# Seven half products in three more places, and the first loads written into the order

## The chip, the cores and the metric

The kernel runs on one core of one Trainium2 chip. The metric is the device time of one execution in microseconds (us), median of the runs. A core has TensorE (PE, the matmuls and the loads of their weights), VectorE (DVE), ScalarE (ACT) and GpSimd (POOL, which here only issues DMAs), each working through its own instructions in program order, and SyncE (SP), which issues the other DMAs. Data goes from DRAM to SBUF and back by DMA; matmuls write to PSUM, which has eight banks of 128 partitions by 2 KB.

## The reference

Two stages. First attention over a short window with a few global positions (4 batches, 8 heads, 768 positions, head size 64):

```python
scores = scale * np.matmul(q, k.transpose(0, 1, 3, 2))
keep = is_global | is_local          # column < 8, or 0 <= row - column < 96
bias = -slopes[:, None, None] * dist[None, :, :]
a = softmax(np.where(keep, scores + bias, -1e9))
attn = np.matmul(a, v)               # written [batch * position, head * 64]: 3072 x 512
```

Then two matrix products with a squared ReLU between them:

```python
h = x @ w_in                         # 3072 x 512 times 512 x 2048
g = np.maximum(h, 0.0) ** 2
out = g @ w_out                      # 3072 x 2048 times 2048 x 512
```

## The kernel before

**Tiles and blocks.** The 3072 positions are 24 tiles of 128 (index j) and 12 blocks of two tiles (blk). A tile needs of attention only itself, the tile in front of it and the global positions. All matmuls are in bf16.

**One tile of attention.** `tr.n.j` and `T.n.j` transpose q (n = 0) and k (n = 1) by PE and copy them out of PSUM (tiles 0 to 5); from tile 6 on one `T.j` does both as a DMA transpose issued by SP. `bias`, `sc.j.g` (scores, in two groups of heads), `exp.j.odd.g` (ACT), `mul.j.odd.g` (DVE, times a table of biases), `pv.j.hf` (PE, times v) and `norm.j.hf` (DVE) follow. `gk`, `gv` and `kl` copy the global positions. The normed tile is transposed for the second stage by `trx.j` and `xT.j` (tiles 0 to 7, PE and a copy) or by `xT.j` alone (from tile 8, a DMA transpose by SP).

**Stage 1 of a block.** `s1.blk.s` for s = 0 to 7 gives 256 of the 2048 hidden columns for both tiles: eight matmuls of 256 columns (one per token of the block) into one bank. `relu.blk.s` (ACT) and `sq.blk.s` (ACT or DVE) follow; in the list, @A and @V name the engine.

**Stage 2 of a block.** Plain (`s2.blk.s.sub`): for each step s and tile of the block two matmuls of 512 columns. In blocks 2 to 10 it is done as seven half products instead, function `seven`: the product is seen as a 2 x 2 product of blocks (two tiles, two halves of each pair of hidden columns, two halves of the 512 output columns). Four sums of the squared activations (`sum.blk.i`, DVE) and four sums of weights (`wsum.i.g`, DVE, made once) let seven products `p1` to `p7` of 8 matmuls of 256 columns stand for eight. They gather in two banks, x and y, of a ring of two (`ps_acc`); `part.blk.p` copies between products, and `o.blk.p` write the output tile, which `st.blk.sub` stores (SP). Block 11 is plain, with its last tile cut at column 384.

**PSUM.** Two banks are the ring `ps_acc`; six are the ring `ps_g` (named g, the score ring) which scores, transposes and stage 1 share in turn.

**Loads.** POOL issues them through `swdge` (line 258), in one queue. q, k and v come as float32 and land as bf16. Thirty-four first loads (tiles 1 to 5, v of tile 0, and all weights: `i` is `win`, `o` is `wout`) are issued by one loop ahead of everything else, from a string in the kernel:

```python
for w in "q1 k1 k3 v0 q2 k2 v1 q3 v2 i0 i1 v3 i2 i3 q4 o0 k5 k4 i4 o1 v4 i5 q5 i6 o2 i7 o3 o4 o5 v5 o6 o7".split():
    pieces[w[0]](int(w[1:]))
```

Behind them come `load.6` to `load.23` (q, k and v of one tile each); `gate.8` to `gate.10` are tiny writes by DVE that hold back the load of the same number.

**What sets the order.** The list ORDER holds one word per piece of work. `Plan.run` emits the pieces in the order of the list, and so it fixes, for every engine and queue, in which order it does its own. The costs and keys given to `plan.op` change nothing of that. Waits between engines follow from the data.

Of the kernel before, what the change touches and what calls it, by code (L numbers as in the profile page):

```python
# [11 lines left out]
FP32 = mybir.dt.float32  # L12
# [42 lines left out]
tr.0.0 T.0.0@A tr.1.0 tr.0.1 T.0.1@A bias.0.0 tr.1.1 T.1.0@V T.1.1@A sc.0.0 bias.1.0 exp.0.0.0 sc.1.0 exp.0.1.0  # L55
bias.1.1 exp.1.0.0 exp.1.1.0 pv.0.0 pv.0.1 norm.0.0 norm.0.1 sc.1.1 tr.0.2 tr.1.2 gk.1 tr.1.3 exp.1.0.1 exp.1.1.1
T.1.2@V bias.2.0 T.0.2@V pv.1.0 T.1.3@A sc.2.0 trx.0 exp.2.0.0 pv.1.1 bias.2.1 xT.0@V exp.2.1.0 tr.0.3 T.0.3@A sc.2.1
gk.2 sc.3.0 exp.2.0.1 sc.3.1 exp.2.1.1 exp.3.0.0 exp.3.1.0 exp.3.1.1 norm.1.0 norm.1.1 trx.1 gv.1 pv.2.0 mul.3.0.0
xT.1@V pv.2.1 s1.0.0 s1.0.0#2 exp.3.0.1 norm.2.0 norm.2.1 mul.3.1.0 gv.2 s1.0.1 mul.3.1.1 relu.0.0 pv.3.0 mul.3.0.1
relu.0.1 pv.3.1 sq.0.0@A s1.0.2 trx.2 norm.3.0 norm.3.1 s1.0.2#2 xT.2@V trx.3 xT.3@A sq.0.1@V gk.3 relu.0.2 s1.0.3  # L60
ones.6 load.6 sq.0.2@V relu.0.3 s1.1.0 sq.0.3@A relu.1.0 E0.1 E0.0 sq.1.0@V s1.1.1 relu.1.1 sq.1.1@V tr.0.4 tr.1.5
s1.1.2 s1.1.3 tr.1.4 T.0.4@A relu.1.2 s2.0.0.0 T.1.5@A s2.0.0.1 sq.1.2@A relu.1.3 sq.1.3@A T.1.4@V sc.4.1 sc.4.0
exp.4.1.1 s1.0.4 s1.1.4 exp.4.0.1 relu.1.4 relu.0.4 s1.0.5 gv.3 mul.4.1.1 exp.4.0.0 sq.0.4@V mul.4.0.0 T.6 s1.1.5
s2.0.1.0 exp.4.1.0 mul.4.1.0 mul.4.0.1 tr.0.5 sq.1.4@A pv.4.0 T.0.5@V s2.0.1.1 pv.4.1 relu.0.5 gk.4 norm.4.0 s2.0.2.0
norm.4.1 load.7 relu.1.5 sc.5.0 exp.5.1.0 sc.5.1 mul.5.1.0 s1.1.7 s2.0.2.1 gv.4 s1.0.6 exp.5.0.0 exp.5.0.1 sq.0.5@A
s1.0.7 sq.1.5@A s1.1.6 s2.0.3.1 s2.0.4.1 s2.0.3.0 relu.1.7 sq.1.7@V wsum.0.0 wsum.1.0 mul.5.0.0 relu.0.7 sq.0.7@A
exp.5.1.1 trx.4 mul.5.0.1 mul.5.1.1 relu.0.6 sq.0.6@A relu.1.6 s2.0.4.0 pv.5.0 xT.4@A s2.0.5.1 wsum.2.0 norm.5.0
s2.0.5.0 pv.5.1 s2.0.6.0 norm.5.1 s2.0.7.0 o.0.0@A s2.0.6.1 s2.0.7.1 trx.5 s2.1.0.1 s2.1.1.1 s2.1.2.1 s2.1.3.1 xT.5@V
sq.1.6@A s1.2.0 st.0.0 s2.1.4.1 gate.8 wsum.0.1 relu.2.0 T.7 wsum.3.0 wsum.2.1 sq.2.0@V load.8 s1.2.2 relu.2.2 s1.2.4
sq.2.2@A s2.1.5.1 s2.1.6.1 o.0.1@V s2.1.7.1 relu.2.4 s1.2.5 relu.2.5 o.1.1@V sc.6.0 exp.6.0.0 st.1.1 exp.6.1.0 s1.2.1  # L70
s2.1.0.0 s1.2.3 sq.2.5@V sq.2.4@A sc.7.0 relu.2.1 st.0.1 mul.6.0.0 sc.7.1 mul.6.1.0 gate.9 exp.7.0.0 s2.1.1.0 s2.1.2.0
s2.1.3.0 T.8 exp.7.1.1 s1.2.7 gk.7 mul.7.0.0 wsum.1.1 wsum.3.1 relu.2.3 mul.7.1.1 exp.7.1.0 mul.7.1.0 load.9 exp.7.0.1
mul.7.0.1 sq.2.1@A pv.6.0 sq.2.3@A relu.2.7 pv.6.1 sq.2.7@A s1.2.6 relu.2.6 s2.1.4.0 s2.1.5.0 load.11 pv.7.1 pv.7.0
norm.6.0 norm.6.1 s2.1.6.0 trx.6 s2.1.7.0 s2.2.p1.0 o.1.0@A norm.7.0 norm.7.1 trx.7 sq.2.6@V xT.6@A xT.7@A T.9 sc.8.1
sc.8.0 sum.2.0 sum.2.1 s2.2.p2.0 exp.8.1.1 exp.8.0.0 s2.2.p1.1 exp.8.0.1 gate.10 s1.3.2 load.10 mul.8.1.1 s1.3.0
sum.2.2 exp.8.1.0 s1.3.4 relu.3.0 part.2.p1@V s2.2.p6.0 mul.8.0.0 mul.8.1.0 s2.2.p2.1 gv.7 pv.8.0 mul.8.0.1 relu.3.2
sq.3.0@V pv.8.1 s2.2.p6.1 norm.8.0 s1.3.1 norm.8.1 gk.8 part.2.p6@A relu.3.4 sq.3.2@A o.2.p2 relu.3.1 xT.8 s2.2.p7.0
s2.2.p5.0 s2.2.p5.1 gv.8 sum.2.3 sc.9.1 sc.9.0 s2.2.p7.1 exp.9.0.1 sq.3.4@V s1.3.5 sq.3.1@V mul.9.0.1 load.12
exp.9.1.1 gk.9 s1.3.3 exp.9.1.0 mul.9.1.1 exp.9.0.0 part.2.p7@V T.10 s2.2.p4.0 T.11 load.13 mul.9.1.0 relu.3.5
relu.3.3 sq.3.3@A pv.9.1 mul.9.0.0 pv.9.0 sq.3.5@V norm.9.0 norm.9.1 s1.3.6 s1.3.7 relu.3.6 o.2.p5 sq.3.6@V s2.2.p4.1  # L80
s2.2.p3.0 relu.3.7 s2.2.p3.1 o.2.p4@V gv.9 sq.3.7@A s2.3.p1.0 s2.3.p1.1 xT.9 o.2.p3 sum.3.0 s2.3.p2.0 st.1.0 sum.3.1
s2.3.p2.1 sc.10.0 sc.10.1 exp.10.0.1 exp.10.0.0 part.3.p1@V o.3.p2 s2.3.p6.0 s2.3.p6.1 s2.3.p5.0 mul.10.0.1 mul.10.0.0
T.12 gk.10 exp.10.1.1 s2.3.p5.1 mul.10.1.1 exp.10.1.0 s1.4.0 relu.4.0 mul.10.1.0 s1.4.6 sum.3.2 pv.10.0 pv.10.1
norm.10.0 sc.11.0 relu.4.6 exp.11.1.0 norm.10.1 xT.10 sq.4.0@V s1.4.7 s1.4.5 load.14 mul.11.1.0 part.3.p6@V sc.12.0
exp.11.0.0 load.15 relu.4.7 sq.4.6@A sum.3.3 mul.11.0.0 sc.11.1 s2.3.p7.0 relu.4.5 exp.11.1.1 exp.11.0.1 sq.4.7@V
mul.11.1.1 s2.3.p7.1 exp.12.0.0 gv.10 exp.12.1.0 part.3.p7@V s1.4.3 T.13 mul.11.0.1 s1.4.2 pv.11.0 mul.12.1.0 pv.11.1
s1.4.1 mul.12.0.0 norm.11.0 relu.4.3 norm.11.1 sq.4.5@A pv.12.0 s1.4.4 xT.11 sq.4.3@A norm.12.0 s2.3.p4.0 relu.4.2
sq.4.2@A s2.3.p4.1 pv.12.1 relu.4.1 st.2.1 relu.4.4 o.3.p5 sq.4.1@V o.3.p4@A s2.3.p3.0 sq.4.4@A st.2.0 s2.3.p3.1
load.16 s2.4.p1.0 norm.12.1 o.3.p3 sum.4.0 s2.4.p1.1 sum.4.1 part.4.p1@V s2.4.p2.0 s2.4.p2.1 sc.13.0 exp.13.1.0
sc.13.1 exp.13.0.0 mul.13.1.0 s2.4.p6.0 s2.4.p6.1 mul.13.0.0 part.4.p6@A exp.13.1.1 exp.13.0.1 sum.4.2 xT.12 s1.5.2  # L90
s1.5.0 s2.4.p7.0 pv.13.0 s2.4.p7.1 T.14 relu.5.0 mul.13.1.1 st.3.0 part.4.p7@A mul.13.0.1 o.4.p2 relu.5.2 s1.5.5
sq.5.0@V s2.4.p5.0 s1.5.3 relu.5.3 sq.5.3@A sq.5.2@V pv.13.1 s1.5.1 s1.5.7 s2.4.p4.0 s2.4.p5.1 st.3.1 norm.13.0 s1.5.4
norm.13.1 relu.5.5 xT.13 sum.4.3 sq.5.5@A T.15 gk.13 s1.5.6 o.4.p5 relu.5.7 gv.13 s2.4.p4.1 relu.5.1 sq.5.7@A sq.5.1@V
relu.5.4 relu.5.6 sq.5.4@A s2.4.p3.0 s2.4.p3.1 load.17 o.4.p4@V s2.5.p1.0 sc.14.1 kl.14 sq.5.6@A load.18 sc.14.0
exp.14.1.0 o.4.p3 s2.5.p1.1 s2.5.p2.0 s2.5.p2.1 sum.5.0 sum.5.1 part.5.p1@A exp.14.0.0 s2.5.p6.0 sum.5.3 mul.14.0.0
exp.14.0.1 mul.14.1.0 s2.5.p6.1 s1.6.0 exp.14.1.1 o.5.p2 T.16 part.5.p6@A pv.14.0 s2.5.p5.0 sum.5.2 relu.6.0 s1.6.6
mul.14.0.1 s2.5.p7.0 relu.6.6 norm.14.0 mul.14.1.1 pv.14.1 norm.14.1 xT.14 sc.15.0 sc.15.1 s1.6.7 s2.5.p5.1 s2.5.p7.1
s1.6.4 sq.6.0@A load.19 exp.15.1.0 kl.15 mul.15.1.0 gv.14 exp.15.0.1 mul.15.0.1 exp.15.0.0 mul.15.0.0 exp.15.1.1
mul.15.1.1 sq.6.6@A part.5.p7@V o.5.p5 relu.6.7 pv.15.0 pv.15.1 norm.15.0 relu.6.4 sq.6.7@A s2.5.p4.0 sc.16.1 sc.16.0
norm.15.1 xT.15 gv.15 exp.16.0.1 gk.16 s2.5.p4.1 s1.6.1 s1.6.3 s1.6.2 s2.5.p3.0 exp.16.1.1 exp.16.1.0 st.4.0 T.17  # L100
relu.6.1 mul.16.0.1 mul.16.1.1 mul.16.1.0 sq.6.4@V exp.16.0.0 mul.16.0.0 pv.16.0 s1.6.5 pv.16.1 s2.5.p3.1 sq.6.1@V
relu.6.3 T.18 s1.7.1 relu.6.2 sq.6.3@A relu.6.5 norm.16.0 o.5.p4@A sq.6.2@V s1.7.0 s2.6.p1.0 sq.6.5@A o.5.p3 st.5.0
s2.6.p1.1 sum.6.0 norm.16.1 xT.16 sum.6.1 load.20 relu.7.0 part.6.p1@A s2.6.p2.0 s2.6.p2.1 relu.7.1 s2.6.p6.0 st.4.1
s2.6.p6.1 sc.17.0 sq.7.0@V sc.17.1 sum.6.2 part.6.p6@A T.19 sc.18.0 o.6.p2 s2.6.p7.0 s2.6.p7.1 exp.17.1.1 exp.17.0.0
s2.6.p5.0 s2.6.p5.1 s1.7.3 exp.17.0.1 sq.7.1@V mul.17.1.1 gv.16 exp.17.1.0 part.6.p7@V sum.6.3 relu.7.3 mul.17.0.0
st.5.1 mul.17.1.0 exp.18.0.0 o.6.p5 s1.7.5 pv.17.0 s2.6.p4.0 mul.17.0.1 s2.6.p4.1 pv.17.1 exp.18.1.0 mul.18.0.0
norm.17.0 mul.18.1.0 s2.6.p3.0 o.6.p4@A s2.6.p3.1 s1.7.4 norm.17.1 xT.17 sq.7.3@V relu.7.5 pv.18.1 sq.7.5@V s1.7.2
pv.18.0 s1.7.6 relu.7.2 norm.18.0 s1.7.7 sq.7.2@V load.22 s2.7.p1.0 relu.7.4 load.21 o.6.p3 sq.7.4@A s2.7.p2.0
norm.18.1 relu.7.7 relu.7.6 sq.7.7@V sq.7.6@A xT.18 sum.7.0 sc.19.1 kl.19 sc.19.0 s1.8.0 exp.19.1.0 mul.19.1.0 T.20
exp.19.1.1 exp.19.0.1 s2.7.p1.1 s1.8.1 s2.7.p2.1 s1.8.2 part.7.p1@A mul.19.0.1 sum.7.1 s2.7.p6.0 s2.7.p6.1 s1.8.4  # L110
st.6.1 sum.7.2 st.6.0 T.21 o.7.p2 exp.19.0.0 mul.19.1.1 mul.19.0.0 pv.19.1 pv.19.0 s2.7.p5.0 relu.8.0 sq.8.0@V
relu.8.1 part.7.p6@V s2.7.p7.0 s1.8.5 s1.8.6 s2.7.p7.1 relu.8.2 sq.8.2@A sq.8.1@V load.23 relu.8.4 norm.19.0 s2.7.p5.1
# [27 lines left out]
def kernel(  # L140
# [13 lines left out]
    P = 128  # L154
# [73 lines left out]
    STEP = {(4, 0): -7, (12, 0): 37, (5, 0): -2, (10, 0): 29, (13, 0): 30, (23, 1): 81}  # L228
    JGATE = 11
    NHB = 3  # L230
    SEVEN = set(range(2, 11))
    SQA = {3, 6}
    NSUM = 2
    NAT = 8
# [5 lines left out]
    LEAD = 12  # L240


    land = {}
    issue = [1.35, 4.6]

    def landed(name, at):
# [914 lines left out]
```

## Time and profile before

| | us |
|---|---|
| median of 3 runs | 207.66 (206.72 to 208.12) |
| the profiled execution | 206.5 |
| its span, first to last instruction | 204.7 |
| PE busy | 197.9 (97%) |
| DVE busy | 146.5 (72%) |
| ACT busy | 142.8 (70%) |
| first matmul of stage 1 (s1.0.0) | 16.55 |
| first matmul of s2.0.6.0, which needs wout 6 | 40.79 |
| last matmul ends | 201.3 |

Times in the profile count from the first instruction of the span. The page names groups by line, engine and operation, with out<-in in the program's names; "x8" is eight instructions. The chain of waits goes back from the last instruction to what released each step. A busy PE there includes the running out of the pipeline after the last matmul, so the start-to-start distances in the chain are the better price of a matmul. Granted clock is the TensorE clock that the throttle let through; it is 1.00 in every stretch.

### The profile page before, as it was taken

How to read it: one execution, taken by the hardware profiler on the slowest of the kernel's cores; microseconds unless marked ns; L12 is line 12 of the kernel's file. 1: busy time of each engine (PE TensorE's matmuls, PEld its weight loads, DVE VectorE, ACT ScalarE, POOL GpSimd, SP SyncE). 2: the span in 40 equal slices, each digit the busy share in tenths (PEclk: the TensorE clock that was granted, in tenths of full speed). 3: DMA queues.
4: the chain of work that ended last, by engine and by line, in shares of the span. 5: the costliest groups of instructions: out<-in, count | busy, mean ns of one | idle time of the engine just before them, and what ended most of it. 6: DMA issues, size and time to landing. Idle time of an engine off the chain costs nothing.

```text
span 204.7 us, 5515 instructions
## 1 busy us (share of the span) xinstructions
PE 197.9 (97%) x2200; PEld 162.6 (79%) x2200; DVE 146.5 (72%) x394; ACT 142.8 (70%) x277; POOL 75.3 (37%) x93
## 2 busy tenths in 40 slices
PE   7988999999999999999999999999999999999993
PEld 3667976657679888888988898989888888989851
DVE  8269736855788997987577978869698778747331
ACT  6986988835986847976787976576859587744330
POOL 8999866540639049150316305180500000000000
PEclk9999999999999999999999999999999999999999
DMA  8999999999999999969997999999985212120032
GB/s 127 151 172 183 182 188 205 181 154 178 213 122 111 166 138 151 153 127 144 191 140 72 108 228 142 164 117 239 145 124 80 52 74 83 29 102 0 5 115 90
DMA packets 113676, 27.36 MB, mean 134 GB/s; under 512 B 105330, under 2 KB 110706, under 8 KB 113650
## 3 DMA queue, kind: packets, MB, share of 16 engines
q0 software_dynamic: 80256, 13.37, 93.5%
q1 hardware_dynamic: 33394, 13.64, 35.3%
q8 instruction: 17, 0.28, 0.5%
q14 instruction: 9, 0.07, 0.1%
HBM read 27.26 MB, written 6.29 MB: 164 GB/s over the span
## 4 chain that ended last, share of the span: by engine, by line
PE 86%; POOL 5%; DVE 3%; DMA 2%; ACT 2%; issue 0%; POOLq 0%; ACTq 0%
PE hT L813 39%; PE acc L951 27%; PE acc L1068 10%; PE sc L538 5%; PE po L691 5%; POOL qk L258 3%; DMA win<-in_moe_w_in_dram 2%; POOL v L258 1%; ACT hr L836 1%; DVE at L629 1%; POOL win L258 1%; PE trx L759 1%; DVE v L739 1%; DVE x L722 0%; ACT esc L604 0%
## 5 line engine op out<-in xcount | busy, mean ns | idle before, releaser
L813 PE MATMUL hT<-xT,win 128*128 128x256 bf16 x768 | 94.4, 273 | 0.1
L813 PEld LDWEIGHTS <-win 128*128 128x128 bf16 x768 | 73.5, 98 | 10.4 <-issue 0.2
L836 ACT ACTIVATE hr<-hT 128x512 f32<-128x512 f32 x96 | 56.3, 602 | 31.1 <-PE hT L813 27.1
L604 ACT ACTIVATE esc<-sc 128x512 bf16<-128x512 f32 x78 | 42.0, 607 | 10.4 <-PE sc L538 10.1
L258 POOL DMA_DIRECT2D qk<-in_q_dram x23 | 20.9, 908 | 65.9 <-DMA qkT<-qk 49.9
L854 DVE TENSOR_TENSOR hs<-hr 128x512 bf16<-128x512 f32 x46 | 31.1, 685 | 9.7 <-ACT hr L836 9.6
L629 DVE TENSOR_TENSOR at<-esc,E 128x512 bf16<-128x512 bf16 x78 | 31.3, 419 | 7.1 <-ACT esc L604 6.1
L852 ACT ACTIVATE hs<-hr 128x512 bf16<-128x512 f32 x50 | 31.1, 635 | 0.7
L951 PEld LDWEIGHTS <-hsum 128*128 128x128 bf16 x288 | 27.0, 98 | 3.5
L951 PE MATMUL acc<-wsum,hsum 128*128 128x256 bf16 x216 | 28.9, 273 | 0.0
L1068 PE MATMUL acc<-wout,hs 128*128 128x512 bf16 (+2 forms) x112 | 24.0, 349 | 0.0
L951 PEld LDWEIGHTS <-hs 128*128 128x128 bf16 x216 | 20.6, 98 | 3.0
L258 POOL DMA_DIRECT2D v<-in_v_dram x24 | 21.9, 913 | 1.0 <-DMA win<-in_moe_w_in_dram 0.6
L722 DVE TENSOR_TENSOR x<-po,rs 128x256 bf16<-128x256 f32 x48 | 20.4, 425 | 1.9 <-DVE rs L721 0.2
L258 POOL DMA_DIRECT2D qk<-in_k_dram x23 | 20.6, 901 | 0.7 <-DMA win<-in_moe_w_in_dram 0.4
L951 PE MATMUL acc<-wout,hs 128*128 128x256 bf16 x144 | 18.9, 273 | 0.0
L691 PE MATMUL po<-v,at 128*128 128x65 bf16 x352 | 17.0, 193 | 0.7 <-DVE v L739 0.3
L691 PEld LDWEIGHTS <-at 128*128 128x128 bf16 x352 | 15.4, 98 | 2.8 <-DVE at L629 0.6
L1018 DVE TENSOR_TENSOR o<-acc,part 128x256 f32<-128x256 f32 x27 | 11.4, 421 | 6.6 <-PE acc L951 6.1
L1068 PEld LDWEIGHTS <-hs 128*128 128x128 bf16 x112 | 9.9, 98 | 6.7
L721 DVE RECIPROCAL rs<-po 128x4 f32<-128x4 f32 x48 | 8.5, 176 | 9.0 <-PE po L691 9.0
L916 DVE TENSOR_TENSOR hsum<-hs 128x1024 bf16<-128x1024 bf16 x18 | 12.2, 684 | 2.4 <-ACT hs L852 2.3
(60 smaller groups left out, 167.5 us busy)
## 6 DMA issues: line engine op xcount, KB each, us to landing
out_dram<-o SPq DMA_DIRECT2D x23, 256.0 KB, 3.3
v<-in_v_dram POOLq DMA_DIRECT2D x24, 128.0 KB, 5.8
qk<-in_q_dram POOLq DMA_DIRECT2D x23, 128.0 KB, 4.7
qk<-in_k_dram POOLq DMA_DIRECT2D x23, 128.0 KB, 5.2
wout<-in_moe_w_out_dram POOLq DMA_DIRECT2D x8, 256.0 KB, 9.4
win<-in_moe_w_in_dram POOLq DMA_DIRECT2D x6, 256.0 KB, 7.7
win<-in_moe_w_in_dram POOLq DMA_DIRECT2D x4, 128.0 KB, 5.2
qkT<-qk SPq DMA_TRANSPOSE x18, 4.8
```

The source lines that it names most:

```text
L258: nc.gpsimd.dma_start(out=dst, in_=src)
L604: nc.scalar.activation(out=esc, in_=tiles.pop(("sc", j, odd, g)).rearrange("p a c -> p (a c)"), func=Act.Exp, scale=scale,)
L629: nc.vector.tensor_mul(at, tiles.pop(("esc", j, odd, g)), bias)
L691: nc.tensor.matmul(out=po[:, hi, :], lhsT=tiles["at", j, odd, g][:, at * P : (at + 1) * P], rhs=v_sb[kj][:, h, :], start=(i == 0), stop=(i ...
L722: nc.vector.tensor_tensor(out=x[:, 4 * hf : 4 * hf + 4, :], in0=po[:, :, :D], in1=rs.to_broadcast([P, 4, D]), op=Alu.mult,)
L813: nc.tensor.matmul(out=hT[:, c, :], lhsT=w_in_sb[s][:, kt, c * P : (c + 1) * P], rhs=tiles["xT", blk][:, kt, :], start=(kt == 0), stop=(kt ...
L836: nc.scalar.activation(hr, tiles.pop(("hT", blk, s)), Act.Relu)
L852: nc.scalar.activation(hs, hr, Act.Square)
L854: nc.vector.tensor_mul(hs, hr, hr)
L916: nc.vector.tensor_tensor(out=t[:, i], in0=t[:, a] if isinstance(a, int) else half_a(blk, *a), in1=t[:, b] if isinstance(b, int) else half ...
L951: nc.tensor.matmul(out=tiles["acc", blk, bank], lhsT=left_[:, s], rhs=w_sum[b][:, s] if isinstance(b, int) else w_part(s, *b), start=first ...
L1068: nc.tensor.matmul(out=tiles["acc", blk, sub, half], lhsT=hs[:, c, sub * P : (sub + 1) * P], rhs=w_out_sb[s][:, c, cols], start=(s == 0 an ...
```

## The change

Four things, and a new list.

1. `SEVEN` becomes blocks 1 to 11: block 1 and block 11 lose their plain stage 2. The sums of weights are so needed one block earlier.
2. In block 11 the two banks of the seven products come from the score ring, the four sums are made in two halves (steps 0 to 3 and 4 to 7, words like `sum.11.0#2`), the last product `p3` is cut at column 192 of its 256, and every finished piece of output is stored by itself.
3. In block 0 the steps s = 0 to 3 are done per tile (128 columns), so that the first half needs only tile 0: `s1.0.0` to `s1.0.0#4`, `s1.0.3#2` and so on.
4. The first loads become words of the list (`ld.k.1`, `ld.win.0.1`, ...), emitted where the list has them; the string only makes them.

```diff
-    SEVEN = set(range(2, 11))
+    SEVEN = set(range(1, NBLK))
+    LASTCUT = 192
+    NTOK = 4
...
+    first_loads = [True]
...
-        nc.gpsimd.dma_start(out=dst, in_=src)
+        if first_loads[0]:
+            land[name] = plan.op(
+                ("ld",) + name, {"LD": t}, lambda e: nc.gpsimd.dma_start(out=dst, in_=src)
+            )
+        else:
+            nc.gpsimd.dma_start(out=dst, in_=src)
...
+            cols = slice(ts[0] * P, (ts[-1] + 1) * P)
...
-                        rhs=tiles["xT", blk][:, kt, :],
+                        rhs=tiles["xT", blk][:, kt, cols],
...
-        for cs in sets:
+        for cs, ts in [(cs, ts) for ts in ([(0,), (1,)] if blk == 0 and s < NTOK else [(0, 1)]) for cs in sets]:
...
+        last = blk == NBLK - 1
+        pieces_ = [slice(0, NSTEP // 2), slice(NSTEP // 2, NSTEP)] if last else [slice(0, NSTEP)]
...
+            cuts = [slice(0, LASTCUT), slice(LASTCUT, HN)] if last and name == "p3" else [slice(0, HN)]
...
+                            pool, tag = (ps_g, "g") if last else (ps_acc, "acc")
+                            tiles["acc", blk, bank] = pool.tile([P, HN], FP32, name="acc", tag=tag)
...
+        quarters = blk == NBLK - 1
...
+                c = cols if quarters else slice(0, d_model)
+                nc.sync.dma_start(out=out[r0 : r0 + P, c], in_=tiles["o", blk, sub][:, c])
```

The new list, cut to the stretches that the prediction speaks of. The whole order of the POOL queue in it is: k1 q1 v0 k2 q2 q3 v1 k3 v2 win0 (two halves) win6 v3 win3 k4 q4 win4 win1 q5 k5 win2 (two halves) load.6 wout0 win5 v4 win7 v5 wout2 wout1 load.7 wout5 wout3 wout4 wout7 wout6 load.8 and on. PE's pieces from s1.1.3 to s2.0.7.0, in order: s1.1.3 sc.4.1 s1.0.4 s1.0.2 s1.1.2 s2.0.0.0 tr.1.5 s2.0.0.1 s1.0.2#2 to #4 s1.0.5 pv.4.0 s1.1.7 pv.4.1 sc.5.0 sc.5.1 s1.1.5 s1.0.7 trx.4 s2.0.1.0 pv.5.0 s1.1.1 pv.5.1 s2.0.1.1 s2.0.2.1 s2.0.2.0 s2.0.3.0 trx.5 s2.0.4.0 s2.0.5.0 s2.0.3.1 s2.0.4.1 s2.0.5.1 s1.2.0 s2.0.6.0 s2.0.7.0.

```diff
+tr.0.0 T.0.0@A ld.k.1 tr.1.0 ld.q.1 tr.1.1 ld.v.0 bias.0.0 ld.k.2 T.1.1@V tr.0.1 T.1.0@A T.0.1@V sc.0.0 bias.1.0
...
+sq.1.4@A relu.0.1 tr.0.5 ld.wout.0 exp.4.0.0 s1.1.3 sq.0.1@V sc.4.1 T.0.5@A s1.0.4 mul.4.0.0 exp.4.1.0 ld.win.5.0 E0.1
...
+mul.5.0.1 s2.0.1.0 mul.5.1.1 pv.5.0 ld.wout.4 norm.5.0 relu.0.7 s1.1.1 ld.wout.7 pv.5.1 norm.5.1 s2.0.1.1 s2.0.2.1
+s2.0.2.0 s2.0.3.0 sq.1.5@V trx.5 s2.0.4.0 s2.0.5.0 s2.0.3.1 s2.0.4.1 wsum.0.0 relu.1.1 ld.wout.6 xT.5@V sq.1.1@V
+s2.0.5.1 sq.0.7@A s1.2.0 relu.2.0 sq.2.0@A wsum.0.1 wsum.2.0 s2.0.6.0 sum.1.0 sum.1.1 s2.0.7.0 s1.2.3 relu.2.3
+wsum.2.1 gate.8 o.0.0@A wsum.1.0 s2.0.6.1 s2.0.7.1 s1.2.6 s2.1.p1.0 T.6 relu.2.6 T.7 s1.2.7 sq.2.3@A sq.2.6@A s1.2.5
...
+mul.15.0.1 mul.15.1.1 relu.6.3 mul.15.1.0 o.5.p5 st.4.0 load.19 sq.6.3@A relu.6.4 pv.15.0 s2.5.p3.0 norm.15.0 relu.6.2
+pv.15.1 o.5.p4@A norm.15.1 sc.16.1 sq.6.2@V sc.16.0 xT.15 s1.6.7 s2.5.p3.1 sq.6.4@A exp.16.1.0 exp.16.0.0 mul.16.1.0
...
+o.10.p3 s2.11.p7.1 part.11.p7@A s2.11.p5.0 s2.11.p5.1 s2.11.p4.0 o.11.p5 st.10.1 st.10.0 sum.11.3#2 st.11.1 s2.11.p4.1
+o.11.p4@V st.11.1#2 s2.11.p3.0 s2.11.p3.1 o.11.p3 st.11.0#2 s2.11.p3.0#2 s2.11.p3.1#2 o.11.p3#2 st.11.0#3
```

## The prediction

> **What bounds the kernel now.** I read the page's busy rows and its chain of waits first, then the chain in order of time around the first weights, then the load queue.
>
> ```profile
> PE 197.9 (97%) x2200; PEld 162.6 (79%) x2200; DVE 146.5 (72%) x394; ACT 142.8 (70%) x277; POOL 75.3 (37%) x93
> ...
> PE 86%; POOL 5%; DVE 3%; DMA 2%; ACT 2%; issue 0%; POOLq 0%; ACTq 0%
> ```
>
> TensorE (PE) sets the end. From 19 us on the chain is one matmul after another; the 5% of POOL and 2% of DMA are the first loads, before that. So a microsecond of PE work saved is a microsecond won, unless PE then waits. Prices per matmul, start to start, from the chain: "0.87 PE hT L813 x8" is 109 ns for 256 columns, "1.73 PE acc L1068 x8" is 216 ns for 512.
>
> What PE can be made to wait for is seen in the DMA view of the window 10 to 46 us, and in the timeline of POOL:
>
> ```profile
> DMA  9999999999999999999999999999999999999997
> ...
> DMA packets 24334, 6.49 MB, mean 180 GB/s; under 512 B 19209, under 2 KB 24329, under 8 KB 24329
> ```
>
> ```profile
> 31.18 0.71 POOL L258 DMA_DIRECT2D wout<-in_moe_w_out_dram  x1 [0.61 <-DMA win<-in_moe_w_in_dram]
> 32.42 0.88 POOL L258 DMA_DIRECT2D qk<-in_q_dram  x1 [0.54 <-DMA wout<-in_moe_w_out_dram]
> ...
> 38.84 0.88 POOL L258 DMA_DIRECT2D v<-in_v_dram  x1
> ```
>
> All 16 DMA engines are full for 36 us, and POOL itself waits for old loads to land before it can issue. The landing times (issue plus the time to landing in the view of the tile) keep the order of issue: v2 8.44 + 4.65 = 13.1, wout 7 (the last first load) 31.18 + 9.6 = 40.8, v7 (the end of load.7) 38.84 + 7.1 = 46.0. The six transfers of load.6 and load.7 fill 40.8 to 46.0: 0.87 us each. From v2 to wout 7 land seven transfers of that kind and 16 weight tiles' worth (four halves counted as two): (27.7 - 7 x 0.87) / 16 = 1.35 us per weight tile. PE uses wout 7 soon after:
>
> ```profile
> 40.96 1.73 PE acc L1068 x8
> 42.68 0.22 PE trx L759 x4
> 42.91 1.73 PE acc L1068 x8
> ```
>
> The first of these pieces is s2.0.6.0, s2.0.7.0, s2.0.6.1, s2.0.7.1 (first matmul 40.79); s2.0.7.0 starts 0.46 us after its weights. So before, the loads are just in time.
>
> **What the change takes from PE.** Block 1: 32 matmuls of 512 columns (6.91) become 56 of 256 (6.10): -0.81. Block 11: 6.96 becomes 48 x 0.109 + 8 of 192 columns (82 ns by columns) + 8 of 64 = 6.12: -0.84. No row has 64 columns; the 65-column po matmuls start every 29 ns in their runs, those of 128 every 56: 8 x 29 to 8 x 56, I take 29, the nearest. The Trainium skill, "TensorE: Matmul & The Clock Gate", section "Wait — 56ns, not 53.3ns?", gives about 62 ns of sequencer time per matmul with hardware decode off; by it these eight would cost 0.26 us more. The po rows at 29 ns, each with its own weight load, disagree, and I go by them. Steps per 128 tokens: 64 matmuls at 56 for 32 at 109: +0.1, and it falls in front of the wait below.
>
> **What the change puts in PE's way.** In the new order the loads are words of the list, and load.6 stands before wout.0, load.7 between wout.1 and wout.5. POOL issues in the order of the list, nothing holds those two back (their slots are fresh), and the queue is full. So six transfers of 0.87 us go ahead of weights that before preceded them. Of the set that landed by 46.0, only wout 7 and wout 6 now come after wout 4: wout 4 lands at 46.0 - 2 x 1.35 = 43.3, wout 3 at 42.0, wout 6 at 46.0. By the same pitches win 2 lands about 25.7, wout 0 after load.6 at 29.6, win 7 at 33.0.
>
> Where PE stands: before, at 27.95 it had done 9 steps of stage 1 and 0.86 us of stage 2 (8.7 us together); the new list has 10.25 steps (8.9 us) ahead of s2.0.0.0. Equal, so PE is there at about 28, and waits for wout 0 until 29.6. From there to s2.0.3.0 are 9.5 us of matmuls, 0.3 of switches to scores and 0.5 of waiting for win 7: ready at 39.9, weights at 42.0. Then trx.5, and s2.0.4.0 waits until 43.3. In all some 5 us of waiting between 28 and 44, where before the rows show under 1. An earlier start of block 0 (s1.0.0 at 15.4 instead of 16.55) is worth nothing: PE has 2 us to spare when it reaches wout 3. All that is behind in PE's queue waits along; DVE waits too, wsum.0.0 for wout 3 and wsum.0.1 for wout 6, with sum.1.0 to wsum.1.0 behind (0.68 each, done about 49.8; s2.1.p6.0 needs them at 53).
>
> **The sum.** From 43.3 five pieces of stage 2 (2.16) and s1.2.0 (0.87): s2.0.6.0 at 46.3, its weights just there. Before it stood at 40.79, with 204.7 - 40.8 = 163.9 us to the end of the span. Of that the new order has less: 0.81 and 0.84 as above, and 1.09 (trx.5 and s1.2.0) that it did earlier. 46.3 + 163.9 - 2.74 = 207.5 against 204.7: +2.8.
>
> Middle: the same 17 runs of scores remain, with their switches. One wait goes (0.27 at 52.2, sc.7.0 behind T.7: T.6 and T.7 now have their data by 39). One comes: pv.15.1 to s1.7.0 is 4.84 us of matmuls plus 0.2, before 6.4 passed. Before, xT.15 was issued 1.2 us after pv.15.1 and landed 4.5 later: 5.7, so +0.7; 0 if it lands in 2.5, as xT.9 did, +2.3 if in 6.2, as xT.10. gate.8 now stands behind wsum.2.1, so load.8 is issued near 49 instead of 43.7; T.8 lands about 59, sc.8 asks at 64: hidden, with 5 us of cover.
>
> Tail: part.11.* and o.11.* (0.37 to 0.42 each) stand between products on two banks. Walking the four queues I find every answer there before PE asks, the closest by 0.25 us (sum.11.3#2 and o.11.p5 before s2.11.p3): 0, up to +0.8. Half sums are not shown; between 0.42 (128x512) and 0.68 (128x1024); 0.42 taken. The last store: before 3.4 us from last matmul to end (copy 0.48, landing 1.85, closing 1.05). Now two short adds, a store 0.4 behind another on SP, and 32 KB; the 64 KB store landed in 1.56, the 192 KB one in 1.85, so 1.3 to 1.85: even, -0.3 to +0.5.
>
> Sum: 2.8 - 0.3 + 0.7, rounded down for the bounds of the last term, +3.1. The profiled execution took 206.5 with a span of 204.7, the median is 207.66; I add to the median: **210.8**.
>
> **Rivals.** *The loads do not bind* (faster): if load.6 and load.7 took nothing from the queue, wout 4 would land at 43.3 - 6 x 0.87 = 38.1; PE, which then waits for nothing, asks for it at 38.2, runs through and reaches s2.0.6.0 at 41.7; 41.7 + 163.9 - 2.74 = 202.9, -1.9: 205.8. For it: the weights would then come just as the new list asks for them (wout 3 at 36.8, asked for at 37.5). Against it: landings in strict order, engines full. It decides at one point, wout 4 before or after some 38.6. *More waits behind the first* (slower still): the DMA transposes take 2.4 to 7.5 us in this trace; by the same walk T.11, xT.9 and xT.15 have under 1 us of cover, and three of them late by 0.8 give 213.2. The clock could bring the same sum: the eight warm-up matmuls of 512 columns at the start took 3.6 us, 427 ns each against 216 later; if PE fell back to that pace after its waits, eight such matmuls would cost 8 x 211 ns = 1.7 us, to 212.5. Against it, PE kept its pace between 5 and 20 us, where it idled in pieces of up to 0.65 us; a piece of 2 us is not in the trace. The Trainium skill, "TensorE: Matmul & The Clock Gate", section "HAM oscillation — how this bites in real kernels", puts the idle time that brings the half clock above some 3.4 us; by it pieces of 2 us would not, and no run here shows it yet. *The products save nothing* (the weight loads, 98 ns each, show through at 109): then +1.65, 212.4; the rows of nine blocks at 109 speak against it.
>
> **Chances.** Loads late 0.72; loads not binding 0.13; more waits, clock or no saving 0.15. Range: first case with its bounds (landing pitch 3% off over 33 us: 1 us; transpose 0 to 2.3; tail -0.3 to +0.8) reaches 208.6 to 212.8; up to 213.2 the third comes in. I leave out the second case. A measurement of this kernel tells about 1% (2.1 us) from no change: faster needs below 205.6, half of the second case: 0.07; slower needs above 209.7, 0.9 of the first and all of the third: 0.80; same 0.13.
>
> **What would show it.** Right: PE idle on DMA wout between 28 and 44, 3 us or more in all, load.6's landing before wout 0's, wout 4 landing near 43, PE seamless behind it with acc of 256 columns in blocks 1 and 11. Wrong: s2.0.6.0 before 43 us; or the time lost after 60 us, on transposes or on the score banks.

## The result and the profile after

| | before | after |
|---|---|---|
| median | 207.89 us (206.72 to 208.56) | **216.56 us** (214.37 to 216.97) |
| ratio | | **1.040**, 95% interval 1.032 to 1.049 |
| the profiled execution | 206.5 | 216.97 |
| its span | 204.7 | 215.2 |
| first matmul of s2.0.6.0 | 40.79 | 54.24 (46.3 predicted) |
| from there to the end of the span | 163.9 | 160.96 |

The kernel became slower, as predicted, but by 8.7 us where 3.1 were predicted; 216.56 lies above the stated range, which ends at 213.2. The last two rows say where: the part behind s2.0.6.0 got shorter, as forecast, and the whole surplus lies ahead of it, in the first loads.

Two stretches of the page after: the busy row and the 40 slices of PE and its clock, then the DMA slices and the chain of waits. A slice is 5.4 us.

```profile
PE 202.1 (94%) x2272; PEld 168.9 (79%) x2272; DVE 149.0 (69%) x404; ACT 146.6 (68%) x289; POOL 75.3 (35%) x93
...
PE   7998963978999999999999999999999999999994
...
PEclk9999998596999999999999999999999999999999
DMA  9999999998297999999899995799789511222023
...
PE 76%; DMA 14%; POOL 8%; issue 1%; DVE 0%; POOLq 0%
```

PE's share of the chain fell from 86% to 76% and that of DMA rose from 2% to 14%. PE is thin in slices 6, 7 and 9 (between 27 and 49 us) and full from slice 10 on. Two things are there that the profile before had not: the clock falls in slices 8 and 10, and the DMA engines have a hole in slice 11, where the first loads are through.

PE's waits name the loads (line waited for: us in total, times, the longest):

```profile
PE hT L826 <- DMA win<-in_moe_w_in_dram: 3.9, 2, 3.6
PE acc L1104 <- DMA wout<-in_moe_w_out_dram: 3.8, 3, 1.8
```

The second line is what the prediction expected: three waits, for wout 0, 3 and 4, of 1.8, 1.4 and 0.7 us. The first is not: 3.6 us for win 7, of which 0.5 was expected. The chain in order of time (start, duration, what) goes on from there:

```profile
27.16 13.78 DMA v<-in_v_dram
40.94 0.29 issue
41.23 8.29 DMA wout<-in_moe_w_out_dram
49.52 0.04 issue
49.56 3.97 PE acc L1104 x10
```

The load of v5 took 13.8 us from issue to landing; in the kernel before the loads of v took 4.0 to 9.2 in its first 60 us. It held POOL, and so wout 4 was issued at 41.2 and landed at 49.52 where 43.3 was predicted. And the ten matmuls behind it took 3.97 us where ten at the price of before take 2.16. POOL's own timeline shows the same (start, duration, in brackets the idle time before and what ended it):

```profile
37.41 0.71 POOL L267 DMA_DIRECT2D wout<-in_moe_w_out_dram  x1 [3.67 <-DMA win<-in_moe_w_in_dram]
41.23 1.47 POOL L267 DMA_DIRECT2D wout<-in_moe_w_out_dram  x2 [3.11 <-DMA v<-in_v_dram]
```

What took the queue's time is in the DMA view of the window 34 to 41 us (slices of 0.18 us, then packets, MB and share of 16 engines of each queue):

```profile
DMA  9999999969921079999999999999999999999999
GB/s 161 158 135 159 251 135 154 118 97 99 31 9 13 7 89 147 149 162 167 149 155 125 105 159 89 79 88 108 103 89 101 74 82 133 130 165 157 172 162 166
...
q0 software_dynamic: 2656, 0.62, 176.1%
q1 hardware_dynamic: 800, 0.20, 44.4%
```

q0 is POOL's queue, q1 SP's. The 0.20 MB of q1 are a DMA transpose, and SP's timeline tells which (first the kernel after, then the kernel before):

```profile
28.51 1.33 SPq L487 DMA_TRANSPOSE qkT<-qk  x1
...
42.51 1.33 SPq L475 DMA_TRANSPOSE qkT<-qk  x1
```

That is T.6. load.6, now early, had landed its k and q by 28.43, and SP, which had nothing to do, issued T.6 at once, into full DMA engines. It landed 12.2 us later; before, it was issued at 42.51, when the loads were nearly through, and took 4.4. Its first packets are seen near 32.7. From 33 to 38 us the records of the two queues stand in nearly equal numbers (in the half microsecond from 33.0 there are 120 packets of loads and 119 of the transpose), and the loads moved 22 to 63 KB per half microsecond, 4 in the hole near 36 us, where they had moved 85 to 98. T.7, from 44.7 to 53.5, held the loads up as well (5 to 44 KB per half microsecond from 47.5 to 52, some 100 before), but its packets outnumber theirs there (84 to 14 in the half microsecond from 49.0).

### The profile page after: what moved, and what is told of

It is laid out like the page before. It is cut to its first block, busy times and chain, and to the rows that moved or that the text cites. A ratio compares the mean times of both kernels' runs of the same rounds, so it can differ in the third digit from the quotient of the medians.

```text
span 215.2 us, 5685 instructions
## 1 busy us (share of the span) xinstructions
PE 202.1 (94%) x2272; PEld 168.9 (79%) x2272; DVE 149.0 (69%) x404; ACT 146.6 (68%) x289; POOL 75.3 (35%) x93
## 4 chain that ended last, share of the span: by engine, by line
PE 76%; DMA 14%; POOL 8%; issue 1%; DVE 0%; POOLq 0%
PE hT L826 33%; PE acc L975 32%; DMA v<-in_v_dram 6%; PE sc L550 4%; DMA wout<-in_moe_w_out_dram 4%; PE po L703 4%; DMA win<-in_moe_w_in_dram 4%; POOL qk L267 3%; PE acc L1104 3%; POOL win L267 2%; POOL v L267 2%; POOL wout L267 0%; DVE o L1051 0%; PE trx L771 0%; POOL pbi L327 0%
## 5 line engine op out<-in xcount | busy, mean ns | idle before, releaser
L826 PE MATMUL hT<-xT,win 128*128 128x256 bf16 (+1 forms) x800 | 95.8, 272 | 3.9 <-DMA win<-in_moe_w_in_dram 3.9
L270 POOL DMA_DIRECT2D qk<-in_q_dram x18 | 16.2, 899 | 74.8 <-DMA qkT<-qk 50.6
L975 PEld LDWEIGHTS <-hsum 128*128 128x128 bf16 x360 | 33.5, 98 | 5.0 <-issue 0.6
L975 PE MATMUL acc<-wsum,hsum 128*128 128x256 bf16 x264 | 34.3, 273 | 0.0
L975 PEld LDWEIGHTS <-hs 128*128 128x128 bf16 x264 | 24.9, 98 | 2.9
L1051 DVE TENSOR_TENSOR o<-acc,part 128x256 f32<-128x256 f32 (+2 forms) x34 | 13.9, 411 | 11.2 <-PE acc L975 9.8
L390 ACT COPY part<-acc 128x256 f32<-128x256 f32 x24 | 9.0, 374 | 15.0 <-PE acc L975 14.6
L270 POOL DMA_DIRECT2D v<-in_v_dram x18 | 16.3, 906 | 0.8 <-DMA win<-in_moe_w_in_dram 0.8
L932 DVE TENSOR_TENSOR hsum<-hs 128x1024 bf16<-128x1024 bf16 (+1 forms) x24 | 15.4, 641 | 1.3 <-ACT hs L865 1.0
L550 PE MATMUL sc<-qkT 64*128 64x128 bf16 x192 | 13.5, 223 | 0.0
```

The lines of the kernel that those rows point to most:

```text
L270: nc.gpsimd.dma_start(out=dst, in_=src)
L550: nc.tensor.matmul(out=tiles["sc", j, odd, g][:, at, :], lhsT=left[j - 1][half, pair, :] if kt else qkT[j % NKT][half, 1, pair, :], rhs=qk ...
L826: nc.tensor.matmul(out=hT[:, c, cols], lhsT=w_in_sb[s][:, kt, c * P : (c + 1) * P], rhs=tiles["xT", blk][:, kt, cols], start=(kt == 0), st ...
L932: nc.vector.tensor_tensor(out=t[:, i, h], in0=t[:, a, h] if isinstance(a, int) else half_a(blk, *a)[:, h], in1=t[:, b, h] if isinstance(b, ...
L975: nc.tensor.matmul(out=tiles["acc", blk, bank][:, cols], lhsT=left_[:, s], rhs=right_[:, cols], start=first and s == 0, stop=s == NSTEP - ...
```

## The experiments

The theory after this comparison: the loads in the new order cost what the prediction had worked out, and T.6 and T.7, which no step of it placed among the loads, cost the rest, partly by the clock that falls when PE waits long. The rivals: the late loads alone are worth more than predicted; or the new middle and tail are slower. The kernels that are compared below ran beside the kernel before on the same chip, and ratios go by that.

**1. load.6 and load.7 behind the weights.**

```diff
-... s1.0.1#2 sc.4.0 load.6 sq.1.4@A ...   /   ... relu.0.5 load.7 relu.1.7 ...
+... wsum.0.0 relu.1.1 ld.wout.6 load.6 load.7 xT.5@V ...
```

> The changed kernel, with the words load.6 and load.7 moved behind ld.wout.6, so that the first weights have the load queue to themselves and T.6 finds its data only after them. Theory (load.6 and load.7 ahead of the weights, and T.6 let loose in the full queue by load.6, are all of the loss; the products and the last block work as counted): wout 6 lands near 41, s2.0.6.0 starts at 41 to 42, granted clock 1.00, time 1 to 2 us under the kernel before (205.5 to 207). Rival 1 (the new order of the weights is itself slow in the queue): wout 6 after 46, time 211 or more. Rival 2 (the products, the score ring or transposes of the middle lose too): wout 6 near 41, but the time from s2.0.6.0 to the end over 162 us, and no gain on the kernel before.

Measured: **204.57 us, ratio 0.988 (0.985 to 0.991)**: 1.2% faster than the kernel before, and below the expected 205.5 to 207. wout 4 landed near 38.4 and wout 6 by 40.95, T.6 ran from 42.71 to 47.14, and from 14.3 us on PE did not wait for a load by more than 0.3 us. The chain:

```profile
36.90 1.73 PE acc L1103 x8
38.62 0.22 PE trx L770 x4
38.84 2.16 PE acc L1103 x10
41.00 0.87 PE hT L825 x8
41.88 0.22 PE acc L1103
```

Here s2.0.1.1 (36.9) to s2.0.6.0 (41.88) run without a gap: ten matmuls take 2.16. So all else in the change is worth a gain, and the place of these two loads, with the transposes that they let go, turns it into a loss. This is the prediction's rival of loads that do not bind, reached by moving the loads away: it put s2.0.6.0 at 41.7 and the span at 202.9. Measured are 202.7 and, by PE's timeline, 41.71. (Where PE runs through, the chain puts a step 0.17 us later than the timeline. The prediction counts by the timeline, as in its 40.79, and so do the comparisons below.)

**2. T.6 and T.7 late.** The loads stay as the change has them.

```diff
-o.0.0@A wsum.1.0 ... s2.1.p1.0 T.6 relu.2.6 T.7 s1.2.7 ... sq.2.5@A st.0.0 s2.1.p2.0
+o.0.0@A st.0.0 T.6 T.7 wsum.1.0 ... s2.1.p1.0 relu.2.6 s1.2.7 ... sq.2.5@A s2.1.p2.0
```

> The changed kernel, with load.6 and load.7 left where they are, but T.6 and T.7 (the DMA transposes on SP) moved behind st.0.0, which waits for the end of block 0's first tile: no transpose runs while the first loads do. Theory (the transpose held up the load queue by 6 us, and the wait of 3.7 us that it made on win 7 dropped the clock): wout 4 lands at 43 to 44 as predicted from the order of loads alone, no wait of PE over 2 us, granted clock 1.00, time 2 to 3.5 us over the kernel before (210 to 211.5). Rival (the loads were slow for another reason, such as POOL issuing late, and T.6 was only its victim): wout 4 after 48, time still 215 to 217.

Measured: **211.04 us, ratio 1.018 (1.013 to 1.022)**, clock 1.00 throughout the profiled execution. The trace has the predicted times to the tenth: wout 4 lands at 43.23 (43.3 predicted), s2.0.6.0 starts at 46.30 (46.3), 46.46 in the chain.

```profile
34.57 8.66 DMA wout<-in_moe_w_out_dram
43.23 0.04 issue
43.27 2.32 PE acc L1103 x10
45.59 0.87 PE hT L825 x8
46.46 0.21 PE acc L1103
```

So the order of the loads costs what the prediction says, and the transposes make the rest: by the ratios (1.040 against 1.018) 4.7 us, and 3.8 by the later runs of the changed kernel (1.036, below). The late transposes have a small price of their own here: at 58.1 the scores of tile 6 wait 0.7 us for T.6.

**3. T.6 alone early.**

```diff
-... o.0.0@A wsum.1.0 ... T.6 relu.2.6 T.7 ... st.0.0
+... o.0.0@A T.6 st.0.0 T.7 wsum.1.0 ... relu.2.6 ...
```

> The changed kernel with T.7 alone moved behind the first store of block 0 on SP's queue; T.6 stays where its data lets it start, near 28.5. Theory A, T.6 among the first loads is what makes the loss that the prediction lacks (216.6 against 211.0 with both late): PE's waits of 3 to 4 us come again and the time is 215 to 217. Theory B, T.7 has a large part in it: 212 to 214.

Measured: 214.21 us, ratio 1.033 (1.029 to 1.037): between the two expectations. wout 4 landed at 48.37, 5.1 later than with both transposes late; wout 6 at 50.92. In the changed kernel wout 6 came 1.0 to 2.0 later still (at 52.91 in its first profile, at 51.92 in one of a later run); these are single profiles. So T.6 is the larger part, 3.2 us by the ratios (1.033 against 1.018), and T.7 with what follows from it the smaller.

**4 to 6. An extra transfer in the kernel before.** One DMA more on SP, 256 KB from SBUF to SBUF, into a tile that nothing reads: the transpose of tile 5's q and k, a plain copy of the same bytes, and the transpose of tile 4's.

```diff
-... mul.4.0.0 T.6 s1.1.5
+... mul.4.0.0 xtra.0 T.6 s1.1.5
...
+nc.sync.dma_start_transpose(out=xtra, in_=qk_ring[slot(5)].rearrange("p n c -> p (n c)"))
```

> The kernel before, plus one DMA transpose of tile 5's q and k (256 KB, into a scratch tile that nothing reads), first on SP: it starts when k of tile 5 and q of tile 5 have landed, near 29.5 us, in the full load queue. Nothing else is changed; its result isn't used. Theory (one transpose in the full queue holds up the loads behind it by 4 to 6 us): it takes over 8 us to land, wout 7 lands at 44 to 47 instead of 40.8, time 3 to 6 us over the kernel before. Rival (a transpose there costs only its bytes, some 1 us of the queue): wout 7 by 42, time 0 to 1.5 us over.

> The same place in the kernel before, but a plain copy of tile 5's q and k (256 KB, SBUF to SBUF) instead of the transpose; its result isn't used either. Theory (it is the transpose's manner of moving that hurts, not a second queue's transfer as such): the copy lands in 2 to 5 us, wout 7 by 42, time 0 to 1.5 us over the kernel before. Rival (any 256 KB on SP's queue in the middle of the loads does it): as the transpose, 3 us and more.

> The kernel before with one DMA transpose more on SP, as in the run with the extra transpose of tile 5, but of tile 4's q and k (which land near 23.6); its result goes to a tile that nothing reads. Question: why T.6 held the load queue up by some 5.5 us in the changed kernel and the extra transpose of tile 5 by only 2.3. Theory A, packets of the two queues take turns one by one, so what a transpose costs the queue depends on how small the load packets are beside it: here they are win 5, v4, q5 and win 6 (win rows of 512 bytes, q and v rows written in 128), no wout rows of 1 KB; the transpose then takes 10 to 12 us and wout 7 lands at 45 to 47 (40.8 before). Theory B, a transpose costs the queue about its own 2.3 us wherever it stands: wout 7 lands near 43, time near 209.5 to 211 as with tile 5.

| extra transfer | issue to landing | wout 7 lands (40.76 before) | time | ratio |
|---|---|---|---|---|
| transpose, tile 5 | 29.45 to 40.2 | 43.04 | 210.83 | 1.014 (1.010 to 1.019) |
| copy, tile 5 | 30.67 to 37.02 | 42.59 | 208.76 | 1.007 (1.004 to 1.010) |
| transpose, tile 4 | 23.86 to 33.70 | 44.46 | 210.57 | 1.016 (1.012 to 1.019) |

One transpose among full loads costs the kernel before some 3 us, with no other edit. It holds the last weights up by 2.3 to 3.7 us. In the first of the three the late weights are not the main part of the loss: T.7 was issued 2.3 us later than before and took 9.4 us to land, where it had taken 7.5, and PE waited longest for that. The waits of PE in that kernel:

```profile
PE sc L538 <- DMA qkT<-qk: 2.5, 1, 2.5
...
PE po L691 <- DMA v<-in_v_dram: 1.1, 1, 1.1
PE acc L1068 <- DMA wout<-in_moe_w_out_dram: 0.7, 1, 0.7
```

The copy's profile is less clean: its loads were already 1.1 us late (win 7 at 34.6 instead of 33.46) before the first packet of the copy, so the copy itself held the queue up by about 0.7. It took 6.4 us to land where 2 to 5 were expected. As a time it costs 1.4 us, less than a transpose (the intervals just touch that of tile 5's); on the queue it costs clearly less only if those 1.1 us are taken off, so that a transpose hurts more than a copy is likely and not shown.

The theory that the loss goes by the size of the load packets beside the transpose has only some support: 3.7 us beside the smaller packets against 2.3, both under the expected 4 to 6, and in neither the 5.1 of T.6. Where T.6 ran alone, both queues together moved 109 GB/s from 33 to 39 us; beside the extra transposes it was 161 (33 to 40) and 173 (28 to 34), and 184 without a transpose in the same 33 to 39 us of run 2. What makes the sum fall so far with T.6 is not settled.

**7 and 8. Waits filled.** Matmuls of zeros in front of the three late steps, so that PE works while it waits; they compute nothing that is used.

```diff
-... s1.1.7 ...   ... s2.0.3.0 ...   ... s2.0.4.0 ...
+... idle.0 s1.1.7 ...   ... idle.1 s2.0.3.0 ...   ... idle.2 s2.0.4.0 ...
...
+for _ in range(n):      # n = 14, 5, 2
+    nc.tensor.matmul(out=fill, lhsT=zero[:, :P], rhs=zero, start=True, stop=True)
```

> The changed kernel with 14, 5 and 2 matmuls of 512 zero columns in front of s1.1.7, s2.0.3.0 and s2.0.4.0, into a bank of the score ring that nothing reads, so that PE works through its waits. The loads stay as late as in the changed kernel. Theory A, the lower granted clock after the 3.7 us wait lies on the path and costs 1.65 us: the clock stays near 1.00 from 35 to 55 us, s2.0.4.0 to s2.0.6.0 takes 3.0 us instead of 4.7, the time falls by 1.2 to 1.9 us against the changed kernel, to 214.5 to 215.3, ratio to the kernel before near 1.035. Theory B, the clock costs nothing on the path, the loads alone make the loss: 216 to 217, ratio 1.04 or above.

> The changed kernel itself, once more, beside the next run on the same chip: 216 to 217 (216.6 in its first runs).

> The changed kernel with the matmuls of zeros in front of its waits, once more, now on one chip with the changed kernel: in the profile of its first run the clock was 1.00 throughout and s2.0.6.0 started at 52.06 instead of 54.24, but its ratio (1.040) was that of the changed kernel. Theory A, the half clock costs 1 to 2 us in most executions of the changed kernel: 1.0 to 2.0 us under the changed kernel's time on this chip. Theory B, the half clock costs that in some executions only, or the loads come later where PE works through: within 0.5 us of the changed kernel.

Measured, first alone: 215.52 us, ratio 1.040 (1.036 to 1.043); then beside the changed kernel: 214.80, ratio 1.033 (1.028 to 1.037), against 215.58, ratio 1.036 (1.031 to 1.041); the changed kernel itself came out below the 216 to 217 expected of it. The clock was 0.997 or more in every run with filled waits, but the gain, 0.8 us, is within what the runs of either scatter; the expected 1 to 2 us did not come. The chain of the changed kernel in its second profile shows why:

```profile
42.29 9.63 DMA wout<-in_moe_w_out_dram
51.92 0.04 issue
51.96 1.02 PE acc L1104 x4
```

Here s2.0.6.0 waits for wout 6, which lands at 51.92, in the middle of T.7, so a slow PE just ahead of it costs nothing. In the first profile the last slow stretch, 49.5 to 52.9, fell behind the landing of wout 4: from the landing of wout 4 to s2.0.6.0 are 4.72 us where run 3 had 3.07, and s2.0.6.0 started 1.3 after wout 6 was there (52.91). The mean clock of a run tells the two kinds apart: at 0.976 to 0.984 the changed kernel took 216.3 to 217.0 (four runs), at 0.992 or more 213.8 to 215.9 (six). Late loads bring both the low clock and a longer time, so the some 2 us between the two kinds need not be the clock's alone. With the waits filled, at full clock, the executions still took 213.5 to 216.2. The clock is a part of the loss in some executions, 1.3 us in the one that was traced, and not the main part.

**9 and 10. Block 11 plain**, in the kernel of run 1.

```diff
-    SEVEN = set(range(1, NBLK))
+    SEVEN = set(range(1, NBLK - 1))
```

The end of the list changes with it: plain pieces for block 11 in place of its products, in two different orders.

> The changed kernel with load.6 and load.7 behind wout 6 (the run at 204.6), and with block 11 done plainly at the end, its last tile cut at column 384, as in the kernel before. It prices the seven products of block 11. Theory A, as the prediction has it, they save PE 0.84 us and the tail costs nothing: about 205.4, ratio to the kernel before 0.991 to 0.993. Theory B, the tail of adds, copies and stores gives the saving back: 204.6 or less, ratio 0.988 or below.

> As the run before with block 11 plain behind well ordered loads, but its end is the order of the kernel before from o.9.p4 on: block 11's first plain pieces stand between the products of block 10, and block 10's stores go out ahead of block 11's. In the run before (208.3) PE waited 0.44 us for a copy between block 10's products, its last matmul ended 1.7 us later than with products, and the two stores of block 10 stood behind the last one of block 11, so that the end came 4.85 us after the last matmul where 3.4 was seen in the kernel before. Theory A, only the saving of the products counts (0.84 us of PE work) and the tail is worth nothing: 205.4, ratio 0.991 to 0.993. Theory B, the end in pieces (seven stores of small parts, the last one 32 KB) is worth something too: 206 or more, ratio 0.995 or above.

Measured: 208.32 (ratio 1.004, 1.002 to 1.007) and 206.46 (0.993, 0.990 to 0.996). The first one, where about 205.4 was expected, had a badly ordered plain end: 0.44 us of waiting between block 10's products and two stores behind the last one. The second has the end of the kernel before, and is the fair price: 206.46 against 204.57, some 1.1 us by the ratios (the two ran at different times, and their intervals leave about 0.9 either way). Its profile had a wait of 1.2 us for win 2 near 24, so the tail is better read by itself. From the first matmul of block 11's stage 1 to the end of the span: 23.62 us in it, 23.65 in the kernel before, 22.67 in run 1, 22.64 in the changed kernel. So the new end, products and small stores together, is worth 0.95 to 1.0 us.

## Why the prediction was right in sign and wrong in size

**What bounds the kernel, and what the loads do: right.** PE bounds it, and the first weights are just in time. Six transfers ahead of the weights make wout 4 land at 43.3, "some 5 us of waiting between 28 and 44": with the transposes out of the way (run 2) wout 4 came at 43.23, s2.0.6.0 at 46.30, and the time was 211.04 for 210.8, or 3.7 us over the kernel before by the ratio where 3.1 were predicted. That the total is so close is partly luck: run 2 has 0.7 us of waiting for T.6 that the prediction lacks, and has not the 0.7 for xT.15 that it counts. The rival's 41.7, met by run 1 at 41.71, is luck too: its own steps (wout 4 asked for at 38.2, then 2.16 and 0.87) give 41.2, and in run 1 PE came to s2.0.4.0 at 38.68.

**The step that failed is the one on T.6 and T.7.** The text says that they "now have their data by 39" and books it as a gain of 0.27. That their data was there was the trouble: k6 and q6 had landed by 28.4, nothing else stood ahead of T.6 in SP's queue, and so a transfer of 256 KB was let loose in the same 16 engines in which the text had just counted each load. The step counted the words that were moved and not what waits for them. In place of the small gain the runs show a loss of 4 to 5 us (ratios of 1.036 to 1.040 against 1.018). "Landings in strict order, engines full" held within POOL's queue; it said nothing of a second queue. The Trainium skill, "DMA: Bandwidth & Descriptors", section "Queues, rings and completion order", has each DMA engine take turns between the queues that have work for it; the nearly equal numbers of packets beside T.6 agree with that, the 84 to 14 beside T.7 are not explained by it alone. A reading of the new order with this rule in hand would have asked what SP issues near 28. The rival of more waits did name transposes, but T.11, xT.9 and xT.15, as work that might come late, and not as what makes the loads late; PE waited for none of these three.

**The clock rival: right as a mechanism, smaller on the path.** The eight matmuls of s1.1.7, after the 3.6 us wait, took 1.68 us instead of 0.87. The text put such a loss at 1.7; on the path it was 1.3 in one profile and nothing in another.

**Behind s2.0.6.0: right in the sum.** 161.2 was predicted to the end, before the terms of the middle and the tail; measured are 161.0 in the changed kernel and in run 1, and 161.7 in run 2. From s2.0.6.0 to block 11's stage 1 the change took 1.97 us (140.29 to 138.32); the text has 0.81 + 1.09 + 0.27 = 2.17, and 0.7 back for xT.15. No wait for xT.15 is in the trace: that term was 0. The bounds that the prediction gives for its range, simply added, reach 214.2 and not 212.8; the measured time lies above either.

**The tail: right in the sum, by two errors.** Block 11's products were to save PE 0.84 and the last store was even. PE saved 0.20 (20.01 us from the first matmul of stage 1 to the last one's end, before 20.21), and the part after the last matmul fell from 3.44 to 2.64. The chain's end in the changed kernel shows the first:

```profile
211.73 0.02 issue
211.75 0.37 DVE o L1051
212.12 0.04 issue
212.17 0.41 PE acc L975 x8
212.58 0.02 issue
212.60 0.22 DVE o L1051
```

The 64-column piece of p3 gathers in the bank that the add of the 192-column piece is just reading, so PE stands for the add: 0.61 us from where the matmuls could have followed. The text found every answer there in time, "the closest by 0.25 us", and names no wait for this pair. Its price of a 64-column matmul was right: they start 28 to 29 ns apart, and 29 was taken. The 62 ns of the Trainium skill, "TensorE: Matmul & The Clock Gate", section "Wait — 56ns, not 53.3ns?", would be 0.27 us more for the eight; the trace does not show that. The smaller last piece then ends sooner: 0.22 us for the add where the copy before took 0.48, and 1.45 to landing for 1.85.

## What to carry to other kernels

A load that is moved forward also moves whatever waits for it: list, for each early load, the instructions that its landing lets go, on every engine and queue, and ask what their own transfers collide with. Where one queue keeps the DMA engines full, a transfer on another queue takes its turns among those packets, and an early DMA transpose is then paid for by the weights behind. A small last piece lets the end come sooner, but where it gathers in the bank that the piece before it is being read from, PE stands for that read (0.61 us here); no run tried it with a bank of its own.

## What the runs showed of the hardware

The half clock comes in stretches of 3.41 us or twice that, on a grid: in the first profile after it runs from 35.88 to 42.70 and from 49.52 to 52.93. Cut along this grid, the table of windows reads (window, length, PE busy, then the other engines, and behind the last bracket the granted clock, the DMA share and GB/s):

```profile
29.06:32.47 3.41, 1.89 (x22) 1.41 (x22) 1.03 (x2) 1.89 (x4) 2.48 (x4) 1.00 1.82 179
32.47:35.88 3.41, 1.14 (x17) 0.94 (x14) 1.64 (x4) 1.76 (x4) 1.27 (x2) 1.00 1.74 160
35.88:39.29 3.41, 2.12 (x16) 1.63 (x16) 0.00 (x0) 0.13 (x1) 0.71 (x1) 0.50 2.04 103
39.29:42.70 3.41, 3.41 (x31) 2.46 (x29) 2.16 (x6) 3.09 (x7) 1.40 (x2) 0.50 2.23 164
42.70:46.11 3.41, 3.41 (x41) 2.57 (x39) 2.21 (x8) 1.03 (x2) 0.70 (x1) 1.00 1.35 201
46.11:49.52 3.41, 1.44 (x9) 0.65 (x8) 1.87 (x5) 1.11 (x2) 0.00 (x0) 1.00 1.29 155
49.52:52.93 3.41, 3.37 (x9) 1.17 (x9) 0.45 (x1) 0.00 (x0) 0.00 (x0) 0.50 0.96 58
```

A window with 1.14 or 1.44 us of work was followed by one at half clock, a window with 1.89 was not, and a full window brought the clock back. The kernel with T.6 alone early and the one with tile 4's transpose say the same: 0.78 and 1.10 us of work, then half clock; 2.06, no half clock. The mark between is not sharp: windows with 1.55 us (run 2, from 40.60) and 1.41 us (tile 5's extra transpose, from 54.97) were followed by the full clock. The Trainium skill, "TensorE: Matmul & The Clock Gate", section "What's actually happening", gives a free-running window of 3413 ns, and the trace agrees. Its section "HAM oscillation — how this bites in real kernels" sums this up as idle gaps above some 3.4 us; here gaps of 2.6 us (T.6 alone) and of 1.36 and 0.65 in one window brought the half clock, and one of 2.5 us that straddles two windows (tile 5's extra transpose, up to 56.8) did not. So the work in a whole window fits these traces better than the length of one gap.

In the changed kernel and in the one with tile 5's extra transpose the DMA engines stood nearly still for 0.5 to 0.7 us while both queues had work (9, 13 and 7 GB/s in the view above, near 36 us; 13, 5 and 7 in the other kernel, near 37). The traces do not show what they waited for.
